# Two products of constants behind each step of the first eight heads, and late lower parts on VectorE

## The chip, the core and the metric

The kernel runs on one core of a Trainium2 chip. The metric is the device time of one execution in microseconds (us). TensorE (PE) runs the matrix products, with its weight loads shown apart (PEld), ScalarE (ACT) the activations and casts, VectorE (DVE) and GpSimd (POOL) the elementwise work, and SyncE (SP) issues every DMA. Each engine works through its own queue in order.

## What is computed

Attention with a memory term for 8 batches and 8 heads (576 tokens, 64 dimensions a head), and on its result a feed-forward layer with SiLU over 4608 tokens (512 to 2048 to 512).

```python
scores = scale * np.matmul(q, k.transpose(0, 1, 3, 2))          # causal mask, row maximum taken off
a = np.exp(scores); a /= a.sum(-1, keepdims=True) + 1e-09
local = np.matmul(a, v)
mem_out = (phi(q) @ M_prev) / (phi(q) @ z_prev + 1e-06)
x = g * mem_out + (1 - g) * local                                # g = sigmoid(beta), one a head
h = x @ w_in                                                     # [4608, 512] x [512, 2048]
out = (h * sigmoid(h)) @ w_out                                   # [4608, 2048] x [2048, 512]
```

## The kernel before

`attention()` is a generator that walks over the 64 heads. For head n it advances `scores` of head n and `values` of head n-1 by one step each per call; ten such steps make a head. `scores` transposes keys and queries on DVE (tile `tt`), lets PE make the scores of four query blocks (L250) and of the last one in two halves (L271), lets DVE mask them and take the row minimum of the negated scores (L252, L284), and ACT take the exponentials (L254, L294). POOL scales the rows (L304). `values` turns these blocks round on PE (L376, L393, L384), ACT copies them out (L401), and PE multiplies them with the memory and the values (L414, L422) into the bank `x`.

The first ten heads (`N_WHOLE`) are made in plain float32: every product of theirs appears as two records of PE. The later heads and the feed-forward layer work in split float32r parts.

Beside the heads, `preparation()` splits the weights, 32 pieces in all, three for every nine steps: for each piece three instructions of DVE on 128x512 (L152, L154, L159), two of POOL (L156, L162) and three of ACT. `ffn()` starts to be written out once the first eight heads are done (`done[0] >= H`), and then takes its share of steps beside the remaining heads. It works in 18 units of 256 tokens. In each unit the hidden activations of 256 columns (bank `h`, L552) pass ACT (tanh, L563), DVE (L564), ACT (upper part `hi`, L567) and POOL (lower part `lo` = th - hi, L568), and then enter the second product (bank `acc`, L532).

The final order of each engine's instructions is made by the framework's scheduler, which starts from the written order and uses a timeline of its own; `tc.issue_after(x)` keeps an instruction behind `x`. So any added instruction moves others as well. The pool `ps_a` holds two banks for `acc`.

Of the kernel before, what the change touches and what calls it, by code (L numbers as in the profile page):

```python
# [33 lines left out]
FFN_RATE = 0.22  # L34
FIRST_RATE = 0.2
FIRST_UNITS = 2
W_EARLY = 2


@with_exitstack  # L40
def memory_attention_then_silu_ffn(ctx, tc, q, k, v, M_prev, z_prev, beta, w_in, w_out, out):
# [173 lines left out]
    def scores(b, h, raw, rest, made, whole):  # L215
# [29 lines left out]
        for i in range(NQ - 1):  # L245
            w = P * i + P
            pt = pool.tile([P, w], F32, tag=f"p{i}", name=f"p{i}", bufs=P_BUFS)
            s = ps_s.tile([P, 512], F32, tag="s", name="s")[:, 0:w]
            for j, (ta, tb) in enumerate(terms):
                nc.tensor.matmul(  # L250
                    s, ta[:, P * i:P * i + P], tb[:, 0:w], start=j == 0, stop=j == len(terms) - 1)
            anchor["dve"] = nc.vector.tensor_tensor_reduce(  # L252
                s, s, mask[:, 3 * P - P * i:], QS, 3.0e38, ALU.add, ALU.min, st[:, i:i + 1]).ins
            nc.scalar.activation(  # L254
                pt, s, AF.Exp, bias=st[:, i:i + 1], scale=-1.0, accum_out=st[:, 10 + i:11 + i])
            pb.append(pt)
            yield
# [82 lines left out]
    def values(b, h, made, xs, whole):  # L340
# [24 lines left out]
        for lo, n, groups in ((0, SPLIT, ((0, 1),)), (SPLIT, HI, ((0, 3), (1, 4), (2,)))):  # L365
            x = ps_x.tile([P, 512], F32, tag="x", name="x")
            started = False
            for group in groups:

                t = ps_t.tile([P, 512], F32, tag="t", name="tp")  # L370
                o, spans = 0, []
                for j in group:
                    q0 = max(P * j, lo)
                    spans.append((j, o, q0 - lo))
                    for i in range(q0 // P, min((lo + n) // P, NQ - 1)):
                        nc.tensor.transpose(t[:, o:o + P], pb[i][:, P * j:P * j + P], ident)  # L376
                        o += P
                    if lo:
                        o += LAST
                if lo:  # L380

                    last, w = pb[-1], o // 2
                    if len(group) == 1:
                        nc.tensor.matmul(  # L384
                            t[:, o - LAST:o + LAST], last[:, 0:P], swapped,
                            start=True, stop=True, is_transpose=True)
                    else:
                        dst = t[:, o - 2 * LAST:o].rearrange("p (a b) -> p a b", b=LAST)
                        if group[1] == NQ - 2:
                            w = HI - P  # L390
                            dst = t[:, o - 2 * w:o].rearrange("p (a b) -> p a b", b=w)[:, :, w - LAST:]
                        c = P * group[0] + P
                        nc.tensor.matmul(  # L393
                            dst, last[:, c:c + P], ident.rearrange("p (a b) -> p a b", b=LAST),
                            start=True, stop=True, is_transpose=True)

                cut = o if group[-1] < NQ - 1 else o - LAST
                ph = pool.tile([P, 512], kind, tag="ph", name="ph", bufs=NB["ph"])
                pp = [ph]
                if whole:  # L400
                    nc.scalar.copy(ph[:, 0:cut], t[:, 0:cut])  # L401
                    if cut < o:
                        nc.scalar.copy(ph[0:LAST, cut:o], t[0:LAST, cut:o])
                else:
                    pl = pool.tile([P, 512], F32R, tag="pl", name="pl", bufs=NB["pl"])
                    nc.scalar.copy(ph[:, 0:o], t[:, 0:o])  # L406
                    nc.vector.tensor_tensor(out=pl[:, 0:cut], in0=t[:, 0:cut], in1=f(ph[:, 0:cut]), op=ALU.subtract)  # L407
                    if cut < o:
                        low = ph[LAST:P, cut:o]
                        nc.vector.tensor_tensor(out=low, in0=t[LAST:P, cut:o], in1=f(low), op=ALU.subtract)  # L410
                    pp.append(pl)
                yield
                if not started:
                    nc.tensor.matmul(x[0:rows, 0:n], ms, qp[:, lo:lo + n], start=True, stop=False)  # L414
                    started = True
                for part in pp:
                    for j, o, q0 in spans:
                        if part is not ph and j == NQ - 1:
                            continue
                        last = part is pp[-1] and group is groups[-1] and j == group[-1]  # L420
                        n_k = LAST if whole and j == NQ - 1 else P
                        nc.tensor.matmul(  # L422
                            x[0:rows, q0:n], vs[0:n_k, j], part[0:n_k, o:o + n - q0], start=False, stop=last)
            if whole:
                nc.scalar.copy(xs[own, lo:lo + n], x[0:64, 0:n])
                yield
                continue
            xb = pool.tile([P, HI], F32, tag="xb", name="xb", bufs=NB["xb"])
            nc.scalar.copy(xb[own, 0:n], x[oth, 0:n])
            nc.vector.tensor_tensor(out=xs[own, lo:lo + n], in0=x[own, 0:n], in1=xb[own, 0:n], op=ALU.add)  # L430
            yield

    xt = {}
    done = [0]

    def attention():
        todo = [(b, h) for b in range(B) for h in range(H)]
# [11 lines left out]
        for n in range(len(todo) + 1):  # L449

            first, made = iter(()), {}
            if n < len(todo):
                first = scores(*todo[n], raws.pop(0), rests.pop(0), made, n < N_WHOLE)
            one = two = True
            m = 0
            while one or two:
                for _ in range(FIRST_STEPS):
                    one = one and next(first, "end") != "end"
                if two and next(second, "end") == "end":
                    two = False  # L460
                    done[0] = n
                if m == 2 and n + 2 < len(todo):
                    raws.append(load_raw(*todo[n + 2]))
                m += 1
                yield
            if n < len(todo):
                b, h = todo[n]
                if n + 2 < len(todo):
                    rests.append(load_rest(*todo[n + 2]))
                if h % 2 == 0:  # L470
                    xt[b, h // 2] = pool.tile([P, S], F32, tag=f"xt{h // 2}", name="xt", bufs=2)
                second = values(b, h, made, xt[b, h // 2], n < N_WHOLE)
# [40 lines left out]
    def ffn():  # L513
# [3 lines left out]
        for u in range(NU):  # L517
# [21 lines left out]
            for p in range(NP):  # L539
# [25 lines left out]
                g = pool.tile([P, 2, 2, T], F32R, tag="g", name="g", bufs=G_BUFS)  # L565
                hi, lo = (g[:, j].rearrange("p c t -> p (c t)") for j in range(2))
                nc.scalar.copy(hi, th)  # L567
                nc.gpsimd.tensor_tensor(out=lo, in0=th, in1=f(hi), op=ALU.subtract)  # L568
                while not {("o", 2 * p), ("o", 2 * p + 1)} <= ready:
                    yield "prepare"  # L570
                before = p, g
# [63 lines left out]
```

## Time and profile before

| | |
|---|---|
| median of 3 runs | 1319.43 us (1318.79 to 1319.77) |
| profiled execution | 1320.44 us device time, span 1318.7 us |
| mean granted clock of PE | 0.971 |
| busy of the span | PE 1272.7 us, DVE 873.2 us, ACT 883.9 us, POOL 868.5 us |

The span runs from the first to the last instruction; 1.7 us lie outside it. A granted clock of 1.00 stands for 2.4 GHz, 0.50 for 1.2 GHz; a value between is a mean over a stretch with both. A busy PE is not PE at its peak: a product that runs at the lower clock is busy for longer. Where the records hold no change of the clock yet, the view shows 1.00; the length of the products themselves then tells the clock.

### The profile page before, as it was taken

The numbers are of one execution on the slowest core, as the hardware profiler recorded it, in microseconds if no ns is written. First come the engines' busy times: TensorE is split into PE (matmuls) and PEld (weight loads), VectorE is DVE, ScalarE is ACT, GpSimd is POOL, SyncE is SP. The second block draws the span as 40 slices with busy tenths as digits, with TensorE's granted clock in tenths as the row PEclk, the third lists the DMA queues.
The fourth block names the chain that finished last, engine by engine and source line by source line (L and its number), as shares of the span: only waits on it lengthen the run. The fifth ranks groups of instructions, "written<-read, shape, count | busy, mean of one in ns | idle before, by whom it ended". The sixth has DMA issues, their size and how long they took to land.

```text
span 1318.7 us, 24662 instructions
## 1 busy us (share of the span) xinstructions
PE 1272.7 (97%) x7858; PEld 1085.1 (82%) x7858; DVE 873.2 (66%) x2436; ACT 883.9 (67%) x2143; POOL 868.5 (66%) x1169
## 2 busy tenths in 40 slices
PE   6989899999999999999999999999999999999998
PEld 2334358888999989998988989899898998998887
DVE  7988874778777778787877777777767674111111
ACT  6777776777787777777777777777777774232222
POOL 6888895777777777777777777777767763221221
PEclk9976679999999999999999999999999999999999
DMA  6766555555455555555455555554545432444444
GB/s 165 190 181 169 158 133 163 141 134 144 127 147 144 138 153 138 153 137 143 133 147 141 136 141 148 137 153 135 156 126 150 121 116 86 154 160 131 144 157 144
DMA packets 302994, 190.39 MB, mean 144 GB/s; under 512 B 258832, under 2 KB 267024, under 8 KB 302864
## 3 DMA queue, kind: packets, MB, share of 16 engines
q1 hardware_dynamic: 302864, 188.82, 51.5%
q8 instruction: 62, 1.02, 0.3%
q14 instruction: 68, 0.56, 0.1%
HBM read 173.02 MB, written 15.73 MB: 143 GB/s over the span
## 4 chain that ended last, share of the span: by engine, by line
PE 73%; DVE 10%; ACT 6%; DMA 3%; issue 3%; POOL 2%; SPq 1%; POOLq 0%; DVEq 0%; ACTq 0%
PE h L552 27%; PE acc L532 24%; PE x L422 7%; PE s L250 5%; PE tp L376 4%; PE x L414 2%; PE tq L351 1%; DVE pl L407 1%; DVE s L252 1%; DVE th L564 1%; ACT p L254 1%; ACT th L563 1%; PE s L274 1%; DVE st L290 1%; DVE tt L221 1%
## 5 line engine op out<-in xcount | busy, mean ns | idle before, releaser
L552 PE MATMUL h<-xu,wi 128*128 128x256 f32 x2592 | 377.7, 287 | 9.3 <-DVE th L564 7.2
L552 PEld LDWEIGHTS h<-xu,wi 128*128 128x128 f32 x2592 | 342.9, 191 | 25.1 <-DVE th L564 9.4
L568 POOL TENSOR_TENSOR g<-th,g 128x512 fp32r<-128x512 f32 x144 | 186.6, 1297 | 203.5 <-ACT g L567 200.2
L532 PE MATMUL acc<-wo,g 128*128 128x512 f32 x864 | 244.7, 398 | 0.2 <-POOL g L568 0.2
L304 POOL TENSOR_SCALAR p<-p,st 128x384 f32<-128x384 f32 (+3 forms) x320 | 182.5, 590 | 76.7 <-DVE st L302 73.7
L532 PE MATMUL acc<-flow,g 128*128 128x512 f32 x864 | 231.2, 394 | 1.3 <-DMA flow<-wo_s 1.3
L564 DVE SCALAR_TENSOR_TENSOR th<-th,h 128x512 f32<-128x512 f32 x144 | 98.4, 684 | 180.3 <-ACT th L563 178.4
L532 PEld LDWEIGHTS acc<-flow,g 128*128 128x128 f32 x864 | 158.8, 188 | 34.4 <-DMA flow<-wo_s 1.8
L254 ACT ACTIVATE p<-s,st 128x128 f32<-128x128 f32 (+3 forms) x256 | 134.9, 528 | 70.7 <-DVE st L252 53.5
L532 PEld LDWEIGHTS acc<-wo,g 128*128 128x128 f32 x864 | 148.7, 189 | 19.7 <-POOL g L568 0.6
L563 ACT ACTIVATE th<-h 128x512 f32<-128x512 f32 x144 | 85.9, 597 | 99.2 <-PE h L552 98.7
L407 DVE TENSOR_TENSOR pl<-tp,ph 128x384 fp32r<-128x384 f32 x216 | 118.6, 551 | 36.0 <-ACT ph L406 32.7
L252 DVE CUSTOM_DVE_ANT_0 s<-s,mask 128x128 f32<-128x128 f32 (+3 forms) x256 | 125.2, 492 | 23.5 <-PE s L250 20.0
L376 PE MATMUL tp<-ident,p 128*128 128x128 f32 x640 | 121.0, 290 | 3.2 <-POOL p L304 2.6
L552 PE MATMUL h<-xu,flow 128*128 128x256 f32 x864 | 122.4, 283 | 0.0
L406 ACT CAST ph<-tp 128x384 fp32r<-128x384 f32 x216 | 104.7, 490 | 26.1 <-PE x L422 21.2
L567 ACT CAST g<-th 128x512 fp32r<-128x512 f32 x144 | 89.2, 620 | 49.1 <-DVE th L564 48.3
L552 PEld LDWEIGHTS h<-xu,flow 128*128 128x128 f32 x864 | 113.1, 191 | 2.3 <-issue 0.3
L376 PEld LDWEIGHTS tp<-ident,p 128*128 128x128 f32 x640 | 81.5, 146 | 27.5 <-POOL p L304 7.2
L422 PE MATMUL x<-pl,vs 128*128 128x256 f32 x324 | 82.1, 308 | 1.0 <-DVE pl L407 0.9
L232 POOL TENSOR_TENSOR kk<-tt,kk 64x576 fp32r<-64x576 f32 x54 | 77.3, 1431 | 5.0 <-ACT kk L230 1.2
L235 POOL TENSOR_TENSOR ql<-tt,qq 64x512 fp32r<-64x512 f32 x54 | 69.8, 1293 | 15.1 <-ACT qq L231 6.7
(103 smaller groups left out, 2399.6 us busy)
## 6 DMA issues: line engine op xcount, KB each, us to landing
flow<-wo_s SPq DMA_DIRECT2D x144, 512.0 KB, 3.6
flow<-wi_s SPq DMA_DIRECT2D x72, 512.0 KB, 3.8
raw<-in_k SPq DMA_DIRECT2D x128, 72.0 KB, 2.5
raw<-in_q SPq DMA_DIRECT2D x128, 72.0 KB, 2.8
out<-o SPq DMA_DIRECT2D x36, 256.0 KB, 4.2
wraw<-in_moe_w_in SPq DMA_DIRECT2D x16, 512.0 KB, 4.4
qn<-in_q SPq DMA_DIRECT2D x64, 128.0 KB, 2.8
vr<-in_v SPq DMA_DIRECT2D x64, 128.0 KB, 2.5
```

The source lines that it names most:

```text
L252: anchor["dve"] = nc.vector.tensor_tensor_reduce(s, s, mask[:, 3 * P - P * i:], QS, 3.0e38, ALU.add, ALU.min, st[:, i:i + 1]).ins
L254: nc.scalar.activation(pt, s, AF.Exp, bias=st[:, i:i + 1], scale=-1.0, accum_out=st[:, 10 + i:11 + i])
L304: nc.gpsimd.tensor_scalar(pb[x], pb[x], st[:, 15 + x:16 + x], 1.0, op0=ALU.mult, op1=ALU.mult)
L376: nc.tensor.transpose(t[:, o:o + P], pb[i][:, P * j:P * j + P], ident)
L406: nc.scalar.copy(ph[:, 0:o], t[:, 0:o])
L407: nc.vector.tensor_tensor(out=pl[:, 0:cut], in0=t[:, 0:cut], in1=f(ph[:, 0:cut]), op=ALU.subtract)
L422: nc.tensor.matmul(x[0:rows, q0:n], vs[0:n_k, j], part[0:n_k, o:o + n - q0], start=False, stop=last)
L532: nc.tensor.matmul(acc[t], ta, tb, start=p == 0 and c == 0 and n == 0, stop=p == NP - 1 and c == 1 and n == len(terms) - 1)
L552: nc.tensor.matmul(h[:, c], ta, tb, start=kk == 0 and n == 0, stop=kk == KD - 1 and n == len(terms) - 1)
L563: nc.scalar.activation(th, h, AF.Tanh, scale=0.5)
L564: nc.vector.scalar_tensor_tensor(out=th, in0=th, scalar=1.0, in1=h, op0=ALU.add, op1=ALU.mult)
L568: nc.gpsimd.tensor_tensor(out=lo, in0=th, in1=f(hi), op=ALU.subtract)
```

## The change

1. `keep_busy` puts two products of 128 x 128 x 128 (float32, the stationary operand is the identity `ident`, the moving one the first 128 columns of `mask`, which are zeros) behind each step of `attention()` while n < 8. They write a bank `idle`, taken from `ps_a` ahead of everything else, which nobody reads. Each pair is kept behind the product that `anchor["pe"]` named before the step. The first two steps of head 0 have no such anchor, so there are 78 pairs, 156 products.
2. Where all heads are written out (`done[0] == B * H`), the lower part of the activated sum is made on DVE and not on POOL: 36 of the 144.

```diff
+WARM = 2
@@ scores: the four query blocks
-                nc.tensor.matmul(
-                    s, ta[:, P * i:P * i + P], tb[:, 0:w], start=j == 0, stop=j == len(terms) - 1)
+                anchor["pe"] = nc.tensor.matmul(
+                    s, ta[:, P * i:P * i + P], tb[:, 0:w], start=j == 0, stop=j == len(terms) - 1).ins
@@ values: the product with the values
-                        nc.tensor.matmul(
-                            x[0:rows, q0:n], vs[0:n_k, j], part[0:n_k, o:o + n - q0], start=False, stop=last)
+                        anchor["pe"] = nc.tensor.matmul(
+                            x[0:rows, q0:n], vs[0:n_k, j], part[0:n_k, o:o + n - q0], start=False, stop=last).ins
+    def keep_busy(behind):
+
+        for _ in range(WARM):
+            with tc.issue_after(behind):
+                nc.tensor.matmul(idle[:, 0:P], ident, mask[:, 0:P], start=True, stop=True)
+
+    idle = ps_a.tile([P, DM], F32, tag="a", name="idle")
@@ attention: each step
+                behind = anchor.get("pe")
                 for _ in range(FIRST_STEPS):
                     one = one and next(first, "end") != "end"
...
+                if behind and n < H:
+                    keep_busy(behind)
@@ ffn
-                nc.gpsimd.tensor_tensor(out=lo, in0=th, in1=f(hi), op=ALU.subtract)
+                late = nc.vector if done[0] == B * H else nc.gpsimd
+                late.tensor_tensor(out=lo, in0=th, in1=f(hi), op=ALU.subtract)
```

What the scheduler makes of it on PE at the very start, the scores of head 0 (`s`, with `tt` and `qf` the keys and queries) and the turning of its feature map (`tq`). Before:

```order
L250 MATMUL s<-tt,qf 128x256
L250 MATMUL s<-tt,qf 128x384
L250 MATMUL s<-tt,qf 128x512
L271 MATMUL s<-tt,qf 64x256
L351 MATMUL tq<-ident,e 128x128 x2
L351 MATMUL tq<-ident,e 64x128
L271 MATMUL s<-tt,qf 64x320
```

And now, where L251 is the old L250, L272 the old L271, L352 the old L351 and L438 an added product:

```order
L251 MATMUL s<-tt,qf 128x256
L438 MATMUL idle<-mask,ident 128x128 x4
L251 MATMUL s<-tt,qf 128x384
L438 MATMUL idle<-mask,ident 128x128 x2
L251 MATMUL s<-tt,qf 128x512
L438 MATMUL idle<-mask,ident 128x128 x10
L272 MATMUL s<-tt,qf 64x256
L438 MATMUL idle<-mask,ident 128x128 x2
L352 MATMUL tq<-ident,e 128x128 x2
L352 MATMUL tq<-ident,e 64x128
L438 MATMUL idle<-mask,ident 128x128 x2
L272 MATMUL s<-tt,qf 64x320
```

Sixteen added products stand ahead of the first half of head 0's last block, four more ahead of the second half.

The same engine where the fourth head begins its turning (`tp` turns blocks `p`, `x` takes products with the values `vr`). Before:

```order
L422 MATMUL x<-ph,vr 64x64
L351 MATMUL tq<-ident,e 128x128 x2
L351 MATMUL tq<-ident,e 64x128
L271 MATMUL s<-tt,qf 64x256
L271 MATMUL s<-tt,qf 64x320
L250 MATMUL s<-tt,qf 128x128
L422 MATMUL x<-ph,vr 64x320
L250 MATMUL s<-tt,qf 128x256
L376 MATMUL tp<-ident,p_654 128x128
```

And now (L423 is the old L422, L377 the old L376):

```order
L423 MATMUL x<-ph,vr 64x64
L438 MATMUL idle<-mask,ident 128x128 x2
L352 MATMUL tq<-ident,e 128x128 x2
L352 MATMUL tq<-ident,e 64x128
L272 MATMUL s<-tt,qf 64x256
L423 MATMUL x<-ph,vr 64x320
L438 MATMUL idle<-mask,ident 128x128 x12
L272 MATMUL s<-tt,qf 64x320
L251 MATMUL s<-tt,qf 128x128
L377 MATMUL tp<-ident,p_713 128x128
```

Twelve of a head's twenty added products stand behind the last product with the values, ahead of the second half of the next scores; the other eight stand in pairs among the turned blocks. The last product with the values has moved ahead of that second half.

The end of PE's queue, the last unit of the feed-forward layer. Before:

```order
L532 MATMUL acc<-wo_142,g 128x512 x6
L552 MATMUL h<-xu,flow 128x256 x12
L532 MATMUL acc<-flow,g 128x512 x6
L532 MATMUL acc<-wo_144,g 128x512 x6
L532 MATMUL acc<-flow,g 128x512 x6
```

And now (L564 is the old L552, L544 the old L532):

```order
L564 MATMUL h<-xu,flow 128x256 x12
L544 MATMUL acc<-wo_142,g 128x512 x6
L544 MATMUL acc<-flow,g 128x512 x6
L544 MATMUL acc<-wo_144,g 128x512 x6
L544 MATMUL acc<-flow,g 128x512 x6
```

Twelve products of the sum before now lie between the last hidden activations and the products that use them, where there were six.

## Rows read from the trace of the kernel before

**Rows 1.** The page: busy tenths and granted clock in 40 slices of 33 us.
```profile
PE   6989899999999999999999999999999999999998
DVE  7988874778777778787877777777767674111111
PEclk9976679999999999999999999999999999999999
```
**Rows 2.** Windows: length, busy of PE, PEld, DVE, ACT, POOL, then clock, DMA share, GB/s.
```profile
16.30:66.10 49.80, 46.19 (x101) 18.42 (x101) 44.31 (x107) 36.97 (x89) 40.18 (x36) 1.00 0.71 190
66.10:176.10 110.00, 98.30 (x286) 44.85 (x285) 95.84 (x213) 83.05 (x201) 93.99 (x86) 0.68 0.58 160
198.00:1318.70 1120.70, 1100.20 (x7354) 1004.06 (x7352) 709.31 (x2049) 740.52 (x1801) 700.91 (x994) 1.00 0.50 141
```
**Rows 3.** Timeline of PE: start, length, what, and the idle time before it with its releaser.
```profile
66.08 0.55 PE L351 MATMUL tq<-ident,e 128*128 128x128 f32 x3
...
76.29 1.87 PE L422 MATMUL x<-ph,vr 128*64 128x320 f32 x8
78.09 0.55 PE L351 MATMUL tq<-ident,e 128*128 128x128 f32 x3
79.65 0.64 PE L271 MATMUL s<-tt,qf 64*64 64x256 f32 x2 [1.01 <-ACT p L254]
80.67 0.75 PE L271 MATMUL s<-tt,qf 64*64 64x320 f32 x2 [0.38 <-ACT p L254]
85.20 0.79 PE L250 MATMUL s<-tt,qf 64*128 64x128 f32 x2 [3.77 <-DVE st L284]
...
98.53 3.44 PE L422 MATMUL x<-ph,vr 128*64 128x320 f32 x8
101.90 0.90 PE L351 MATMUL tq<-ident,e 128*128 128x128 f32 x3
...
116.96 3.37 PE L422 MATMUL x<-ph,vr 128*64 128x320 f32 x8
120.26 0.55 PE L351 MATMUL tq<-ident,e 128*128 128x128 f32 x3
```
**Rows 4.** Windows between changes of the clock, columns as in rows 2.
```profile
82.60:103.00 20.40, 17.80 (x44) 8.60 (x45) 19.96 (x43) 15.45 (x35) 18.02 (x18) 0.50 0.74 208
106.60:120.00 13.40, 13.40 (x35) 6.52 (x35) 11.74 (x24) 9.15 (x24) 10.88 (x9) 0.50 0.50 126
```
**Rows 5.** Timeline of PE, later.
```profile
172.76 3.44 PE L422 MATMUL x<-ph,vr 128*64 128x320 f32 x8
176.12 0.90 PE L351 MATMUL tq<-ident,e 128*128 128x128 f32 x3
...
178.00 3.57 PE L552 MATMUL h<-xu,wi 128*128 128x256 f32 x15
```
**Rows 6.** Waits of DVE, 16.3 to 176.1: us in total, times, longest.
```profile
DVE pair L284 <- PE s L271: 10.3, 10, 1.8
DVE s L252 <- PE s L250: 3.1, 4, 1.6
```
**Rows 7.** Timeline of PE at the start.
```profile
10.30 3.35 PE L250 MATMUL s<-tt,qf 64*128 64x384 f32 x4 [1.67 <-ACT p L254]
13.89 1.11 PE L271 MATMUL s<-tt,qf 64*64 64x256 f32 x2 [0.25 <-ACT p L254]
16.32 0.90 PE L351 MATMUL tq<-ident,e 128*128 128x128 f32 x3 [1.31 <-POOL e L334]
```
**Rows 8.** Groups by shape: busy, mean ns, idle before. POOL from 1090, DVE 198 to 1090.
```profile
L568 POOL TENSOR_TENSOR g<-th,g 128x512 fp32r<-128x512 f32 x37 | 47.8, 1295 | 154.9 <-ACT g L567 154.8
L407 DVE TENSOR_TENSOR pl<-tp,ph 128x512 fp32r<-128x512 f32 x52 | 35.4, 681 | 2.7 <-ACT ph L406 2.2
```
**Rows 9.** Timeline of the end, all engines.
```profile
1311.54 1.29 POOL L568 TENSOR_TENSOR g<-th,g 128x512 fp32r<-128x512 f32 x1 [5.62 <-ACT g L567]
...
1312.89 0.74 PE L532 MATMUL acc<-wo,g 128*128 128x512 f32 x2 [0.17 <-POOL g L568]
```

## The prediction

> **What bounds the kernel now.** I read the slices of the page first: PE is busy nine tenths or more of nearly every slice, but its granted clock is below full in slices 3 to 6, and PE and DVE both have gaps in the first six [rows 1]. So the span falls into two parts. From 198 us to the end PE is busy 1100.2 of 1120.7 us at a clock of 1.00 [rows 2]: this part is bound by PE, both edits leave its useful products alone, and it is shorter only if it starts sooner. The first part, 16.3 to 176.1 us, makes the first eight heads in 159.8 us. There PE is busy 46.2 + 98.3 = 144.5 us, DVE 44.3 + 95.8 = 140.2 us and POOL 40.2 + 94.0 = 134.2 us [rows 2], so three engines lie within 8% of each other and none is the clear bound.
>
> But PE's 144.5 us are swollen. The eight products with the values take 3.37 us from start to start (98.53 to 101.90) in one head and 1.80 us (76.29 to 78.09) in another [rows 3]: the factor 1.87 is the clock. In 82.6 to 103.0 and 106.6 to 120.0 the granted clock is 0.50, that is 1.2 GHz [rows 4]. From one turning of the feature map to the next (the L351 rows) the fast head takes 78.09 - 66.08 = 12.0 us, the next one 101.90 - 78.09 = 23.8 us, of which 5.2 us are waits [rows 3].
>
> What PE did before the clock moved: it rose at 103 and at 120 us, each time behind the run of eight products with the values (98.53, 116.96), which load all 128 rows of the array, and it fell after the waits of 1.01, 0.38 and 3.77 us that lie between 78.6 and 85.2 us [rows 3, 4]. Such a run does not always do it: the one at 172.76 is followed by another slow turning, 0.90 us as at 101.90, not 0.55 [rows 3, 5]. Being busy alone did not raise the clock either: from 106.6 to 120.0 PE was busy 13.40 of 13.40 us at 0.50 [rows 4]. The Trainium skill (TensorE: Matmul & The Clock Gate, Part 1) says that the array is throttled by default and that sustained activity releases it. Read as busy time, the trace differs: that stretch was all busy and stayed at 0.50. By the page alone, filler would have nothing to lift there and would only cost, which is the third rival's sum.
>
> **The change, part by part.**
>
> *The price of one added product.* No product of this shape stands in the trace. The nearest rows are the runs of eight, seven times 128 columns in two passes each (320, 192, 320 and 64 columns): 1.80 / 7 = 0.26 us at full clock, 3.37 / 7 = 0.48 us at half [rows 3]. So 156 products cost 41 us of PE at full clock and 75 us at half. Both ends are kept; I take 0.26, except at the start. Unlike the products with 64 rows (the `64*64` and `64*128` rows), the added ones load 128 x 128, as the turned blocks do. That the moving operand is all zeros has no row; the turned blocks move the identity, which is nearly all zeros, and are not set apart by any row.
>
> *The clock, 16.3 to 176.1 us.* I take it that the added products, which close the gaps and load all rows, hold the clock high for most of this part. Then the eight heads are 8 x 12.0 = 96 us of PE, and the 138 added products that are left for this part (18 of the 156 stand ahead of the first turning) 138 x 0.26 = 36 us: 132 us, against 144.5 before. DVE with 140.2 us is then the most loaded engine, and what the change is worth is what DVE stops waiting for. DVE idles 159.8 - 140.2 = 19.6 us in this part, and PE ends 10.3 + 3.1 = 13.4 us of it [rows 6]. This is the upper bound of the gain. The lower bound is below nothing (second rival). Since PE turns from the most loaded engine into one with 28 us of room, I take two thirds of 13.4: **-9 us**. The rest I leave, because twelve of a head's twenty products stand straight ahead of the second L271 half, for whose result DVE's L284 waits.
>
> *The start.* At the start the clock is low: at 10.30 two blocks of 384 and 512 columns take 3.35 us [rows 7], and 896 columns in two passes take 3.37 us in the slow run above. Four added products, 4 x 0.48 = 1.9 us, fall into the wait of 1.67 us ahead of 10.30. Two and ten more, 12 x 0.48 = 5.8 us, stand ahead of the first L271, which began at 13.89 [rows 7]. Behind it the wait of 1.31 us (L351) gives some of it back, and if the clock rises inside the run of ten, the rest is shorter. Bounds 0 and 5.8; I take half: **+3 us**.
>
> *The lower part on DVE.* On POOL one takes 1295 ns; DVE's nearest subtraction of the same size, with one operand in PSUM, takes 681 ns [rows 8]. The 0.6 us of each count only where PE waits: at the end that is 0.17 us, at 1312.89 [rows 9]. Everywhere else the next block's products cover the chain. Bounds 0 and -0.6; I take **-0.2 us**. DVE has the room: its slices at the end are 1 tenth busy [rows 1]. Twelve products instead of six now lie between the last hidden activations and their use, which covers that chain as well, so nothing new is late there.
>
> *The bank and the order.* `idle` holds one of two `acc` banks, but its last product stands in PE's own queue ahead of head 8, before any sum is begun: 0. Each anchor also moves other instructions. For the order after 198 us the bound is PE's idle time there, 1120.7 - 1100.2 = 20.5 us; I put a few us either way into the range and none into the sum. No DMA is added; loads come a little earlier with the heads.
>
> *The sum:* -9 + 3 - 0.2 = -6.2 us on the profiled execution's 1320.4 (span 1318.7 and 1.7 around it) is 1314.2. That execution stands 1.0 above the median of the runs, 1319.4, so the forecast is **1313 us**.
>
> **The rivals.**
>
> *1. What the clock gives, the filler takes: about 1319.* DVE is busy 19.96 of 20.40 us in the slow stretch from 82.6 [rows 4], so there a faster PE gives almost nothing. If this is the rule, the -9 shrinks to -3 and the start takes it back. Against it: in 106.6 to 120.0 DVE has 1.7 of 13.4 us idle.
>
> *2. Slower, because a run of twelve stands ahead of what DVE needs: 1332.* PE now idles 159.8 - 144.5 = 15.3 us in this part, 1.9 us a head; the twelve are 3.1 us at full clock and 5.8 at half. What exceeds the wait that stood there delays L271, then L284 and, DVE being in order, the weight pieces and row minima queued behind it. At 3.1 - 1.9 = 1.2 us for each of eight heads that is 10 us, with 3 at the start 13 us. It decides as soon as the twelve cost more than about 2 us a head net. For it: the wait of 3.77 us in front of L250 is ended by L284, so delay on PE and delay on DVE feed each other. Against it: that same wait is the place that the run fills.
>
> *3. The products do not lift the clock: 1365.* Then they cost 75 us, less the 15.3 us of waits and some 12 us at the start that can hold them: +45 us or more. For it: the zeros, and 13.4 us of full busyness at 0.50.
>
> *4. The whole of DVE's waits goes and the start is free: 1306.* -13.4 and 0.
>
> **How the numbers follow.** Forecast (1307 to 1316) 0.42, rival 4 0.10, rival 1 0.20, rival 2 0.20, rival 3 0.08. A measurement of this kernel tells 0.2%, 2.6 us, from no change. Faster by more than that: 0.42 + 0.10 = 0.52; same: 0.20; slower: 0.20 + 0.08 = 0.28. The range 1303 to 1335 leaves out about 0.04 below and 0.15 above (rival 3 and the upper third of rival 2).
>
> **What the profile after would show.** Right: L438 in runs of eight to twelve at 0.26 us each; a granted clock of 0.9 or more in slices 3 and 4; the runs of eight at 1.8 us; DVE's waits for L271 and L250 at a third of 13.4 us; the first big block of L552 products, now at 178.0 us [rows 5], some 6 us earlier and everything behind it shifted alike. Wrong: added products of 0.48 us with the clock at 0.50 (rival 3); L284's wait for L271 longer than 10.3 us (rival 2); DVE's idle time unchanged with PE at full clock (rival 1); the stretch from the first big L552 block to the end longer or shorter than before by more than 3 us, in which case the order, which I put at nothing, had a price.

## The result and the profile after

The changed kernel took 1328.28 us (median of 4 runs, 1325.14 to 1329.22) against 1319.11 us for the kernel before on the same chip (4 runs, 1318.03 to 1319.77). The ratio is 1.0057, 95% interval 1.0037 to 1.0077: slower, where I forecast 1313 us and faster. Of every kernel's executions, one more than 1.5% above its fastest is left out; that is one of the six of e8 below. The profiled execution took 1327.76 us, with a span of 1325.7 us and a mean granted clock of 0.983 (before: 0.971).

The page of the kernel after, in 40 slices of 33 us, to hold against [rows 1]:

```profile
PE   7999979999999999999999999999999999999998
DVE  6999984778687768777776767767867775322222
PEclk9799989999999999999999999999999999999999
```

The clock did what I had forecast: slices 3 to 6 were 7, 6, 6 and 7 tenths, and are now 9, 9, 9 and 8. Windows of the kernel after, between turnings of the feature map (columns as in [rows 2]):

```profile
20.96:65.69 44.73, 41.59 (x166) 24.10 (x165) 40.54 (x90) 32.87 (x78) 35.10 (x31) 0.77 0.72 189
65.69:171.72 106.03, 99.42 (x499) 59.11 (x497) 99.33 (x210) 81.50 (x194) 95.84 (x84) 0.97 0.62 177
171.72:198.33 26.61, 19.74 (x92) 13.89 (x90) 20.51 (x50) 17.10 (x42) 23.76 (x28) 0.81 0.39 96
198.33:1325.70 1127.37, 1105.91 (x7376) 1009.76 (x7374) 732.88 (x2089) 743.62 (x1806) 654.88 (x959) 1.00 0.50 140
```

From the turning of head 2 to that of head 8 the clock is 0.97 (before 0.68 [rows 2]). The eight heads take 44.73 + 106.03 = 150.76 us from the first turning to the ninth, against 159.8: 9.0 us less. But the next step, from the turning of head 8 to that of head 9, takes 26.61 us, of which PE is busy 19.74 us. The same step of the kernel before, in one window:

```profile
176.12:193.36 17.24, 17.24 (x89) 11.89 (x88) 12.29 (x32) 11.77 (x31) 16.91 (x19) 0.84 0.62 165
```

There PE was never idle. So of the 9.4 us that this step grows by, 6.9 us are PE's idle time and 2.5 us longer busy time. I cut the two spans at five marks: the turnings of heads 0, 8 and 9, the thirteenth output copied out of `acc` by ACT (at 662.36 us before and 672.49 us after), and the end. The loss is then 4.6 us ahead of the first turning, -9.0 in the eight heads, +9.4 from turning 8 to turning 9, +5.2 from there to the thirteenth output (474.2 us, not 469.0, of which PE is idle 9.7 and not 7.0) and -3.1 from there to the end (653.2 us, not 656.3): +7.0 us, as the spans have it.

Timeline of PE of the kernel after at that step, where the feed-forward layer comes in (L564 is the old L552):

```profile
169.92 1.87 PE L423 MATMUL x<-ph,vr 128*64 128x320 f32 x8
171.72 0.55 PE L352 MATMUL tq<-ident,e 128*128 128x128 f32 x3
174.00 0.39 PE L564 MATMUL h<-xu,wi 128*128 128x256 f32 x1 [1.73 <-ACT xu L516]
176.68 3.20 PE L564 MATMUL h<-xu,wi 128*128 128x256 f32 x14 [2.28 <-DVE xu L517]
179.81 0.97 PE L272 MATMUL s<-tt,qf 64*64 64x256 f32 x4
...
185.68 1.73 PE L564 MATMUL h<-xu,wi 128*128 128x256 f32 x12 [2.86 <-DVE th L576]
...
198.33 0.55 PE L352 MATMUL tq<-ident,e 128*128 128x128 f32 x3
```

And of the kernel before, at the same place:

```profile
176.95 1.11 PE L271 MATMUL s<-tt,qf 64*64 64x256 f32 x2
...
181.49 0.77 PE L271 MATMUL s<-tt,qf 64*64 64x320 f32 x2
...
185.90 1.68 PE L552 MATMUL h<-xu,wi 128*128 128x256 f32 x12
...
193.36 0.55 PE L351 MATMUL tq<-ident,e 128*128 128x128 f32 x3
```

After the change both halves of the scores of head 8 (L272) stand behind the fifteen L564 products, and these wait for `xu`: 1.73 + 2.28 us. Before, the first half stood ahead of them (176.95). Twelve more L564 products wait 2.86 us for `th`. These three waits are the 6.9 us that PE is idle. What DVE does meanwhile, in its timeline:

```profile
168.47 1.75 DVE L155 SCALAR_TENSOR_TENSOR wy<-wraw,wy 128x512 uint32<-128x512 uint32 x1
...
170.54 1.78 DVE L155 SCALAR_TENSOR_TENSOR wy<-wraw,wy 128x512 uint32<-128x512 uint32 x1
...
172.31 0.68 DVE L160 SCALAR_TENSOR_TENSOR wy<-wraw,wy 128x512 f32<-128x512 f32 x1
...
176.14 1.46 DVE L517 TENSOR_TENSOR xu<-xt,xu 128x256 fp32r<-128x256 f32 x3
...
180.71 0.42 DVE L285 CUSTOM_DVE_ANT_0 pair<-s,mask 64x256 f32<-64x256 f32 x1 [1.49 <-PE s L272]
...
194.67 0.57 DVE L253 CUSTOM_DVE_ANT_0 s<-s,mask 128x384 f32<-128x384 f32 x1 [3.94 <-PE s L251]
```

And `xu` on DVE in the kernel before (L517 is the old L505):

```profile
175.15 0.56 DVE L505 TENSOR_TENSOR xu<-xt,xu 128x256 fp32r<-128x256 f32 x1
...
176.24 2.13 DVE L505 TENSOR_TENSOR xu<-xt,xu 128x256 fp32r<-128x256 f32 x2
```

Here PE has come early and DVE has not. Turning 8 comes 4.4 us sooner than before, but pieces of the weights, row minima and row sums stand ahead of `xu` in DVE's queue. DVE begins `xu` at 176.14 us, where it began at 175.15 before, and is done with it at 177.6 us (176.14 + 1.46), where it was done at 178.4. So PE's lead of 4.4 us ends in 4.0 us of waiting for `xu`, and the half of the scores that filled the time before stands behind it now. Then DVE waits 1.49 and 3.94 us for scores that stand behind the L564 products on PE.

DVE's waits for PE in the eight heads, to hold against [rows 6] (13.4 us in all):

```profile
DVE pair L285 <- PE s L272: 5.2, 5, 1.7
DVE s L253 <- PE s L251: 1.1, 2, 0.8
```

They are 6.3 us, 7.1 us less. DVE's idle time in the eight heads fell from 19.6 to 10.9 us (150.76 - 40.54 - 99.33), and its busy time stayed (139.9 and 140.2 us). The start, against [rows 7], and the added products of the whole kernel as one group (two records each, so 156 products in 52.7 us):

```profile
8.54 2.07 PE L438 MATMUL idle<-mask,ident 128*128 128x128 f32 x8
...
15.28 4.63 PE L438 MATMUL idle<-mask,ident 128*128 128x128 f32 x20
19.84 0.64 PE L272 MATMUL s<-tt,qf 64*64 64x256 f32 x2
...
20.96 0.49 PE L352 MATMUL tq<-ident,e 128*128 128x128 f32 x3
```

```profile
L438 PE MATMUL idle<-mask,ident 128*128 128x128 f32 x312 | 52.7, 316 | 0.0
```

Of these, the ones in the eight heads (busy of PE and PEld, clock, DMA share, GB/s):

```profile
20.96:171.72 150.76, 44.24 (x278) 36.98 (x276) 0.91 0.65 181
```

And the late lower part on DVE, against [rows 8, 9]: its group, and the last of them with the products that use it.

```profile
L581 DVE TENSOR_TENSOR g<-th,g 128x512 fp32r<-128x512 f32 x36 | 24.9, 695 | 22.4 <-ACT g L579 22.3
```

```profile
1317.92 0.69 DVE L581 TENSOR_TENSOR g<-th,g 128x512 fp32r<-128x512 f32 x1 [0.69 <-ACT g L579]
...
1319.08 1.54 PE L544 MATMUL acc<-wo,g 128*128 128x512 f32 x6
```

### The profile page after: what moved, and what is told of

Its sections match the earlier page's. It is cut to its first block, busy times and chain, and to the rows that moved or that the text cites. A ratio compares the mean times of both kernels' runs of the same rounds, so it can differ in the third digit from the quotient of the medians.

```text
span 1325.7 us, 25266 instructions
## 1 busy us (share of the span) xinstructions
PE 1280.6 (97%) x8170; PEld 1116.6 (84%) x8170; DVE 904.1 (68%) x2472; ACT 885.6 (67%) x2143; POOL 824.9 (62%) x1133
## 4 chain that ended last, share of the span: by engine, by line
PE 72%; DVE 12%; ACT 5%; POOL 4%; DMA 3%; issue 3%; SPq 0%; POOLq 0%; DVEq 0%; ACTq 0%
PE h L564 28%; PE acc L544 24%; PE x L423 6%; PE s L251 5%; PE tp L377 4%; PE idle L438 1%; DVE st L291 1%; DVE wy L155 1%; PE x L415 1%; PE tq L352 1%; DMA flow<-wo_s 1%; DVE s L253 1%; DVE wy L160 1%; DVE wy L153 1%; POOL p L305 1%
## 5 line engine op out<-in xcount | busy, mean ns | idle before, releaser
L564 PE MATMUL h<-xu,wi 128*128 128x256 f32 x2592 | 377.7, 288 | 12.8 <-DVE th L576 8.1
L564 PEld LDWEIGHTS h<-xu,wi 128*128 128x128 f32 x2592 | 343.2, 191 | 28.0 <-DVE th L576 7.9
L544 PE MATMUL acc<-wo,g 128*128 128x512 f32 x864 | 242.4, 397 | 0.0
L544 PE MATMUL acc<-flow,g 128*128 128x512 f32 x864 | 231.8, 395 | 1.1 <-DMA flow<-wo_s 1.1
L544 PEld LDWEIGHTS acc<-flow,g 128*128 128x128 f32 x864 | 158.3, 188 | 34.0 <-DMA flow<-wo_s 2.4
L581 POOL TENSOR_TENSOR g<-th,g 128x512 fp32r<-128x512 f32 x108 | 140.3, 1299 | 49.8 <-ACT g L579 48.4
L544 PEld LDWEIGHTS acc<-wo,g 128*128 128x128 f32 x864 | 149.2, 188 | 19.4 <-POOL p L308 0.5
L564 PE MATMUL h<-xu,flow 128*128 128x256 f32 x864 | 126.2, 287 | 0.0
L377 PE MATMUL tp<-ident,p 128*128 128x128 f32 x640 | 117.2, 280 | 1.8 <-ACT ph L402 0.8
L564 PEld LDWEIGHTS h<-xu,flow 128*128 128x128 f32 x864 | 115.9, 195 | 2.3 <-issue 0.8
L377 PEld LDWEIGHTS tp<-ident,p 128*128 128x128 f32 x640 | 80.2, 143 | 17.6 <-POOL p L305 2.1
L423 PE MATMUL x<-pl,vs 128*128 128x256 f32 x324 | 82.1, 308 | 2.5 <-DVE pl L408 2.4
```

Of the source, the lines that this page charges most:

```text
L423: anchor["pe"] = nc.tensor.matmul(x[0:rows, q0:n], vs[0:n_k, j], part[0:n_k, o:o + n - q0], start=False, stop=last).ins
L544: nc.tensor.matmul(acc[t], ta, tb, start=p == 0 and c == 0 and n == 0, stop=p == NP - 1 and c == 1 and n == len(terms) - 1)
L564: nc.tensor.matmul(h[:, c], ta, tb, start=kk == 0 and n == 0, stop=kk == KD - 1 and n == len(terms) - 1)
L581: late.tensor_tensor(out=lo, in0=th, in1=f(hi), op=ALU.subtract)
```

## The experiments

Twelve kernels ran, four to a batch, each with five rounds against the kernel before (medians 1319.4, 1319.3 and 1319.5 us in the three batches). Behind the scheduler an instruction that nobody counts on can be taken out or put in while every other one keeps its place; so products and order can be told apart.

**e1: the late edit alone.**

```diff
-                nc.gpsimd.tensor_tensor(out=lo, in0=th, in1=f(hi), op=ALU.subtract)
+                late = nc.vector if done[0] == B * H else nc.gpsimd
+                late.tensor_tensor(out=lo, in0=th, in1=f(hi), op=ALU.subtract)
```

> Only the second edit: no products, no idle bank; the lower part on VectorE once all heads are written out. In the changed kernel the outputs of the units lag those of before by 10.7 us at 1134 us and by 7.0 us at the end, so 3.7 us were won behind 1134 us. Theory A (the late edit and the order of the tail that comes with it win by themselves): 1316 us, 1315 to 1317. Theory B (the lag shrank because the late start had left slack that the tail took back): 1319, no difference to before.

Measured: 1317.64 us, ratio 0.9979 (0.9967 to 0.9992). By the ratio that is -2.8 us, not -0.2 (between the medians 1.8). The order is that of before up to 1106 us; from there on the edit and the new order of the tail come together, so this is the price of both. In its profiled execution the stretch from the thirteenth output to the end is 652.6 us, against 656.3.

**e2: the products alone**, with the lower part left on POOL (the reverse of the diff of e1, in the changed kernel).

> Only the first edit: the 156 products and their bank; the lower part stays on GpSimd. Theory A (the two edits are independent): the changed kernel's time plus the 3 us that the late edit wins, 1330 us, 1328 to 1332. Theory B (no gain from the late edit): 1327.

Measured: 1328.71 us, ratio 1.0075 (1.0059 to 1.0090). The products and what they bring carry the whole loss.

**e3: the order of the changed kernel without its products.** Taken out behind the scheduler: 137 of the 156, all on which no other instruction counts.

```diff
+    mine = [n for n, i in enumerate(rows) if i.opcode == "Matmult" and "idle" in i.outs[0].memref]
+    free = [n for n in mine if rows[n].sync_info is None]
+    for n in reversed(free):
+        del rows[n]
```

> The changed kernel with 137 of its 156 products taken out behind the scheduler, so that every engine keeps the order of the changed kernel; the 19 left are those whose count other engines wait for. Theory O (the new order of the useful work is what costs, above all where the feed-forward layer begins): as slow as the changed kernel or slower, 1325 to 1333, with the granted clock at 0.50 again in the heads and the waits for xu and th at 172 to 186 us still there. Theory P (the products' own time on TensorE costs): back at 1314 to 1319.

Measured: 1327.63 us, ratio 1.0059 (1.0037 to 1.0081). The loss is all there without the products. In its trace (1331.14 us, the longest of its six) the clock over the eight heads is 0.70, and they take 164.6 us; with the products (after) it was 0.91 and 150.8 us. Against e1 the spans differ by 12.1 us (1329.4 and 1317.3), of which 8.8 us lie in the step from turning 8 to 9 (24.0 and 15.1 us) and 2.8 us between there and the thirteenth output. In that step PE, never idle in e1, is idle 4.5 us, for `xu` and `th`, and busy 4.3 us longer, at a clock of 0.79 in place of 0.99. So in this order the held clock does shorten the heads, by 14 us in these two executions. But with the products the first turning is 4.6 us later, the step from turning 8 to 9 takes 26.6 and not 24.0 us, and the stretch behind it is 2.3 us longer; 3.7 us are left between the two spans (1329.4 and 1325.7), and nothing between the medians. The bank `idle` is taken here too, so this run does not tell it from the order; but e6 and e9 below take it as well and are faster than before.

**e4: the products in the order of the kernel before**, 136 of them put in behind their anchors once it had been scheduled, from the first turning on, into a bank that is free then.

```diff
...
+    for name in sorted(new, key=place.get, reverse=True):
+        for i in new[name]:
+            rows.insert(place[name] + 1, i)
```

> The kernel before in its own order on every engine, with 136 of the products put in behind the scheduler, each directly behind the product that the changed kernel ties it to, from the first turning of head 0 on (the pairs ahead of it are left out). They write the bank of the first sum, free then. Theory O (the order costs, the clock gains): 1313 to 1318, clock near 1.00 in the heads and the feed-forward layer beginning a few us before 178. Theory P (the products' time costs): 1322 to 1330. Theory F (VectorE and GpSimd set the pace of the first heads, so that a faster TensorE gives nothing): 1318 to 1321 with the clock near 1.00 and VectorE's waits for TensorE gone but its instructions longer.

Measured: 1328.11 us, ratio 1.0065 (1.0049 to 1.0080). Here the products themselves are at fault: 8.7 us in the order of before. Waits of DVE in the eight heads, which take 170.5 us (L286, L273, L254 and L252 are the old L284, L271, L252 and L250):

```profile
DVE pair L286 <- PE s L273: 17.4, 9, 6.0
DVE s L254 <- PE s L252: 9.3, 6, 3.0
```

That is 26.7 us, twice the 13.4 of [rows 6]: my second rival, in an order that the scheduler had not made for the products.

**e5: 84 products only where PE waited**, in the order of e1.

```diff
+                if i == 0 and j == 0 and 2 <= H * b + h <= H:
+                    AHEAD[made_now.name] = 8
...
+                if x0 == 0 and 1 <= H * b + h < H:
+                    AHEAD[made_now.name] = 4
...
+            rows.insert(place[name], i)
```

> The order of the kernel before (with the late edit), 84 products put in behind the scheduler only where PE waited in its trace: four ahead of the first L271 half of heads 1 to 7 and eight ahead of the first L250 block of heads 2 to 8, 84 x 0.26 = 22 us of PE. Left out against the whole change: the products among the turned blocks and the scheduler's new order. Step 1's theory (the clock held high shortens PE, DVE stops waiting, and the end follows): the late edit's 1317.6 less 5 to 9, 1308 to 1313, clock 0.98 or more. Theory D (DVE and POOL set the pace of the early heads, so a faster PE gives the end nothing): 1316 to 1319, the clock risen all the same. Theory P (products in the old order delay what DVE waits for): 1321 to 1328, DVE's waits for L250 and L271 longer than 13.4 us.

Measured: 1316.70 us, ratio 0.9977 (0.9968 to 0.9987), within the interval of e1. The products cost nothing there, and give nothing: no part of the 5 to 9 us that my theory asked for. Theory D is the one that has this time, with the clock risen: of the nine turnings of heads 0 to 8 seven run at the full clock (0.49 or 0.55 us for the three products, 0.85 or 0.90 at half), three in e1. In the profiled executions the eight heads take 160.9 us against 164.0, a difference that two executions of one order can have (see below the table).

**e6: one product a step** (78), scheduled anew; **e7: products through ten heads** (196); **e8: products of 64 columns.**

```diff
-WARM = 2
+WARM = 1
```

> The change with one product a step and not two (78 in all), scheduled anew. Theory per product (each product costs): half of the loss, 1322 to 1324. Theory O (the loss is the price of the order that the scheduler made, and any other order has a price of its own, not in proportion to the products): not bound to half; 1314 to 1332, and if it falls outside 1321 to 1325 it speaks for O. In its trace the turning of head 8 and of head 9 tell where: O expects the difference in single turnings, not evenly over the eight heads.

```diff
-                if behind and n < H:
+                if behind and n < N_WHOLE:
```

> The change with products behind the steps of the first ten heads and not eight (196 in all). Theory E (the 9.3 us lost between the turnings of heads 8 and 9 come from the lower clock and the waits of PE there, which more products would close): the step from turning 8 to turning 9 falls from 26.6 to about 18 to 20 us, the clock there 0.95 or more, and the time is 1319 to 1323. Theory O (the order at the entry to the feed-forward layer is what costs, products or not): 1326 to 1333, with the clock risen and the step still 24 us or more.

```diff
-                nc.tensor.matmul(idle[:, 0:P], ident, mask[:, 0:P], start=True, stop=True)
+                nc.tensor.matmul(idle[:, 0:P // 2], ident, mask[:, 0:P // 2], start=True, stop=True)
```

> The change with products of 64 columns and not 128, scheduled anew: as many products in about the same places, but some 20 us of PE less in all. Theory per column (PE's time in the products is the price): 1319.4 + 4 to 5, about 1324. Theory O (the order is the price): the time is that of its own order, which differs from the change's in a third of PE's rows: 1316 to 1332, not bound to 1324. Theory D (DVE and POOL set the pace): the eight heads from turning 0 to turning 8 take 148 to 154 us as in the change, though PE has 20 us less to do.

Measured: e6 1312.96 us, ratio 0.9950 (0.9936 to 0.9964); e7 1334.42, ratio 1.0115 (1.0098 to 1.0132); e8 1332.09 (five executions, 1329.53 to 1343.01), ratio 1.0125 (1.0088 to 1.0162). Half the products do not cost half the loss: the kernel is 6 us faster than before, 4.7 us faster than e1, which no price per product can do. Theory E fails too: in e7 the step from turning 8 to 9 is still 24.9 us, and PE is idle in it 1.9 us and no longer 6.9. The clock there is 0.86, not the 0.95 of the theory.

e8 is not the test that I had meant, since a product of 64 columns is not cheaper than one of 128. In e8, eight products (two records each) at the full clock, and twelve at half:

```profile
85.57 2.00 PE L438 MATMUL idle<-mask,ident 128*128 128x64 f32 x16
...
164.86 5.38 PE L438 MATMUL idle<-mask,ident 128*128 128x64 f32 x24
```

That is 0.25 and 0.45 us a product; twelve of 128 columns in the changed kernel take 0.25 each:

```profile
86.54 2.94 PE L438 MATMUL idle<-mask,ident 128*128 128x128 f32 x24
```

And they held the clock less well: the turnings of heads 0, 1 and 6 run at half, and the eight heads take 180.8 us in the profiled execution, one of its two long ones (1343.0 us). So e8 has an order of its own and part of its filler at the lower clock, a piece of my third rival, and tells nothing of either alone.

What e6 does at the entry, on PE and then on DVE:

```profile
169.47 0.90 PE L352 MATMUL tq<-ident,e 128*128 128x128 f32 x3
170.02 2.48 PE L564 MATMUL h<-xu,wi 128*128 128x256 f32 x15
172.43 0.76 PE L272 MATMUL s<-tt,qf 64*64 64x256 f32 x4
...
185.07 0.55 PE L352 MATMUL tq<-ident,e 128*128 128x128 f32 x3
```

```profile
168.77 1.25 DVE L517 TENSOR_TENSOR xu<-xt,xu 128x256 fp32r<-128x256 f32 x3
```

The same fifteen L564 products stand ahead of the same L272, but `xu` is written by 170.0 us, 7.6 us sooner than in the changed kernel (2.3 us of that are the earlier turning), and PE does not wait for it. The step takes 15.6 us, and the eight heads 151.2, as in the change.

**e9: the order of e6 with 62 of its 78 products taken out**, as in e3.

> The kernel with one product a step (1313.0 us), its order kept on every engine, with 62 of its 78 products taken out behind the scheduler (16 stay, on which others count). Theory O (that order is what is better): with the products gone the time stays near 1313, 1310 to 1316. Theory C (it is the clock, held high by few products in the gaps): the clock falls back in slices 3 to 6 and the time goes to 1316 to 1322, that of before or of the late edit alone.

Measured: 1312.72 us, ratio 0.9961 (0.9946 to 0.9975). The clock did fall back, as theory C asks (the middle of its executions has a mean granted clock of 0.973, of e6 0.979, of the kernel before 0.975), and the time did not: the order alone is what is better in e6. Against e1 this is 4.9 us between the medians, but the intervals of the two ratios overlap (0.9946 to 0.9975, 0.9967 to 0.9992). Its profiled execution was the longest of its 12, 1321.3 us, so its row in the table below says little of the others.

**e10 to e12: products for head 0 alone (16), for head 7 alone (20), for heads 4 to 7 (80).** The diff of e10; the others have `n == 7` and `4 <= n < H`.

```diff
-                if behind and n < H:
+                if behind and n == 0:
```

> The change with products behind the steps of head 0 alone: 16 products, 4 to 8 us of PE, most of them in the wait at the start; but the scheduler's order differs from that of the late edit alone in some 2960 rows of PE. Theory per product: the late edit's 1317.6 plus 1 to 3, 1318 to 1321, with a first turning later by 1 to 4 us and nothing else. Theory O: a time of its own, anywhere from 1308 to 1336; outside 1314 to 1324 it can be no price of 16 products.

> The change with products behind the steps of head 7 alone: 20 products, 5 us at the full clock, and the order of before up to turning 7 (it differs from the late edit's in some 800 rows of PE from there on). Theory per product: 1317.6 plus 0 to 5. Theory O: turnings 0 to 7 as in the kernel before within 4 us, and what differs comes at the entry to the feed-forward layer or behind it; the time 1310 to 1332.

> The change with products behind the steps of heads 4 to 7: 80 products, the order of before up to turning 4, and only some 290 rows of PE differ from the late edit's in all. Theory C (the clock is worth something where the order stays): heads 4 to 7 take 4 to 8 us less than the 74 to 76 us of before and the time is 1310 to 1315. Theory D (VectorE and GpSimd set the pace of these heads): 1316 to 1320. Theory P (the products delay VectorE): 1321 to 1326.

Measured: e10 1338.34 us, ratio 1.0145 (1.0131 to 1.0160); e11 1319.90, ratio 1.0010 (0.9997 to 1.0022), which decides nothing; e12 1327.74, ratio 1.0064 (1.0046 to 1.0081). A kernel with sixteen more products, all over by 20 us, is 19 us slower: no price of theirs can do that. That it is their order is so concluded and not shown, since no run has this order without them. The clock of e10 is as low as before (0.66 over the eight heads; before 0.68 from the turning of head 2 on), and PE waits for `xu` at the entry as in the change:

```profile
PEclk8675679999999999999999999999999999999999
```

```profile
174.35 0.38 PE L564 MATMUL h<-xu,wi 128*128 128x256 f32 x1
178.01 3.36 PE L564 MATMUL h<-xu,wi 128*128 128x256 f32 x14 [3.27 <-DVE xu L517]
...
200.13 0.55 PE L352 MATMUL tq<-ident,e 128*128 128x128 f32 x3
```

e12 lies in none of the ranges of its three theories. It has the order of before up to turning 4 and from there on another, on DVE above all, so its heads 4 to 7 hold the clock, the 80 products and a new order together. Window of e12 from turning 4 to turning 8, and below it that of the kernel before:

```profile
103.73:177.66 73.93, 68.49 (x324) 39.76 (x322) 56.92 (x127) 52.22 (x127) 55.59 (x52) 0.91 0.54 153
```

```profile
101.90:176.12 74.22, 67.86 (x191) 30.84 (x190) 63.95 (x143) 55.47 (x135) 64.42 (x59) 0.66 0.54 150
```

A clock of 0.91 in place of 0.66, and the same 74 us: PE is busy 68 us either way, in e12 20.6 us of it with the added products. What the clock gave, the filler took, as my first rival said, here with room left on DVE. But the changed kernel has the same 80 products there and takes 67.4 us (104.28 to 171.72), so in another order it is not so. What e12 loses against e1 lies in the step from turning 8 to 9 (24.0 and 15.1 us). Among its twelve executions the shortest (1320.8 us) has the highest mean clock (0.992) and the longest (1333.8 us) the lowest (0.983); which of the two is the cause, no run tells.

**All kernels at the same marks** (us of the profiled executions; `late` says whether the late edit is in, "full clock" how many of the turnings 0 to 8 run at the full clock):

| kernel | late | full clock | first turning | heads 0 to 7 | turning 8 to 9 | to the 13th output | to the end |
|---|---|---|---|---|---|---|---|
| before | no | 4 | 16.3 | 159.8 | 17.2 | 469.0 | 656.3 |
| after | yes | 9 | 21.0 | 150.8 | 26.6 | 474.2 | 653.2 |
| e1 | yes | 3 | 16.4 | 164.0 | 15.1 | 469.1 | 652.6 |
| e2 | no | 9 | 21.0 | 150.7 | 26.5 | 471.8 | 655.1 |
| e3 | yes | 5 | 16.4 | 164.6 | 24.0 | 471.9 | 652.6 |
| e4 | no | 6 | 16.6 | 170.5 | 15.1 | 469.3 | 654.9 |
| e5 | yes | 7 | 16.4 | 160.9 | 16.5 | 468.7 | 652.5 |
| e6 | yes | 7 | 18.3 | 151.2 | 15.6 | 472.9 | 653.3 |
| e7 | yes | 8 | 21.2 | 156.3 | 24.9 | 478.4 | 652.4 |
| e8 | yes | 6 | 20.8 | 180.8 | 17.1 | 469.8 | 652.5 |
| e9 | yes | 5 | 16.6 | 159.5 | 17.1 | 473.4 | 652.8 |
| e10 | yes | 5 | 20.2 | 152.6 | 27.3 | 478.0 | 659.4 |
| e11 | yes | 4 | 16.3 | 161.9 | 19.4 | 472.4 | 652.5 |
| e12 | yes | 6 | 16.3 | 161.3 | 24.0 | 468.8 | 653.4 |

e1 has the order of before in its first three columns and differs by 4 us in the second, so a difference of that size there is that of two executions. The column "turning 8 to 9" falls into two groups, 15 to 17 us and 24 to 27 us, with e11, which is neither faster nor slower, between them. All of the second (after, e2, e3, e7, e10, e12) are slower than before; of the first, only e4 and e8 are, and they lose it in the eight heads. In every kernel of the second group PE waits for DVE's `xu` at the first large block of L564, 1.7 to 3.5 us; in none of the first group, nor in e11, does it wait there. The number of turnings at the full clock goes with neither group.

## Why the prediction was wrong, step by step

- **The step that failed: "The bank and the order", which I put at nothing.** With the late edit and with 19 of the 156 products left, the new order takes 1327.63 us (e3); the late edit alone 1317.64 (e1). So the order costs 10.0 us, more than the whole change does. The 19 are not it: they all lie ahead of turning 8, where e3 is as fast as e1 (first turning 16.4 us in both, then 164.6 and 164.0 us). I had bounded "the order after 198 us" by PE's idle time there, and had looked for runs of products ahead of L271 up to 176 us; the place that costs most is the one between, 176 to 198 us, which stands in none of my terms. My list of signs did name it: the stretch from the first big L552 block to the end, longer by more than 3 us, is 8.3 us longer (from 178.00 us before, from 176.68 us after).
- **The clock, -9 us.** The mechanism is as I said: the clock rose to 0.97, DVE's waits for PE fell by 7.1 us of 13.4 (to 6.3 us, not to my third, 4.5), and the eight heads took 9.0 us less. But none of it is found at the end. In three pairs of runs with the same order, the products leave the time where it was: 1327.63 without and 1328.28 with them (e3, after), 1312.72 and 1312.96 (e9, e6), 1317.64 and 1316.70 (e1, e5); of the turnings at full clock there are 5 and 9 in the first pair, 3 and 7 in the last. In the fourth (before, e4) they cost 8.7 us, with 4 and 6 such turnings. In the first pair the heads won 14 us in the profiled executions, and the start (4.6 us), the step at the entry (2.6 us) and the stretch behind it (2.3 us) took most of it back; at the entry PE is earlier than the engine that feeds it. One reading was off and enters no term: the clock fell at 82.6 us, inside the wait of 3.77 us (81.4 to 85.2) and not behind it. That the -9.0 matches the forecast to the decimal says little: the same stretch is 152.6 us in e10, at a clock of 0.66.
- **The price of a product, 0.26 us.** 0.25 us at the full clock, as I took it, but 52.7 / 156 = 0.34 us on the mean: in the eight heads 44.2 us where I had put 36, since some ran at the lower clock.
- **The start, +3 us:** +4.6 us, within its bounds of 0 and 5.8.
- **The late edit, -0.2 us, was mis-sized:** -2.8 us (-1.1 to -4.4 by the interval of e1), with the order of the tail that comes with it. The lower part went from 1295 to 695 ns as forecast. I counted one wait at the very end; the stretch from the thirteenth output to the end is 1.5 to 4 us shorter in every kernel with the edit but e10 than in those without it. In which of its blocks those microseconds lie, and whether the edit or the order of the tail wins them, is open.
- **The rivals.** The first (the filler takes what the clock gives) is what heads 4 to 7 of e12 look like, in an order of their own, and not those of the change. The second (runs of twelve delay DVE) is true of the old order (e4) and not of the scheduler's own, where DVE's waits fell; that its 1332 us lies nearest to the measured time is chance. The third (the clock is not lifted) is out by the page of the profile after. A rival that was missing: the scheduler's answer to more products anywhere is a new order for all that follows, and the kernels made so lie between -5 us (e6, e9) and +21 us (e10) of e1.
- **What stays open:** why the scheduler puts the pieces of the weights ahead of `xu` in one order and behind it in another, and how much of the 10 us that one place is. The step from turning 8 to 9 has 9.4 of the 19.2 us (4.6 + 9.4 + 5.2) that the profiled execution lost, and 8.8 of the 12.1 us between those of e1 and e3; what stretches the part behind it (5.2 us in the change, 2.8 in e3) was not followed. Moving `xu` alone was not tried, since other engines count on each instruction around it.

The best kernel of the study is e6, or e9 with the same order: 0.995 and 0.996 of the time before, from an order found by chance and the late edit.

## What to carry to other kernels

Where a scheduler writes the order, an edit has two prices, that of the added work and that of the new order, and the second can be the larger by far: sixteen products came with 19 us here, and another order was 5 us faster than e1. Hold the order and change the work, then hold the work and change the order, before believing either; and put the spread of a few harmless variants into the range of the forecast. Here an engine that was made faster ahead of a hand-over waited there for what the other side did not have ready: look at the first wait behind the stretch, not only at the stretch.

## What the runs showed of the hardware

That products whose moving operand is all zeros and whose results nobody reads raise the granted clock was open ahead of the run; it rose from 0.68 to 0.97 over six heads, and with the order held (e3, after) from 0.70 to 0.91 over eight (in e3 the first 20 us of these lie ahead of the first record of the clock and count as 1.00).

The same instruction of DVE takes from 0.67 to 1.70 us. In the kernel before, one line of the weight pieces from 16.3 to 176.1 us (shortest, middle and longest in ns):

```profile
L154 DVE SCALAR_TENSOR_TENSOR wy<-wraw,wy x29: 674/741/1699, 24.2 to 170.3; 128x512 uint32<-128x512 uint32 x29
```

In the rows of the changed kernel above, where it is L155, it starts at 168.47 and at 170.54 and takes 1.75 and 1.78 us; POOL's rows at these times are

```profile
168.32 1.35 POOL L236 TENSOR_TENSOR ql<-tt,qq 64x512 fp32r<-64x512 f32 x1
...
170.48 1.29 POOL L157 TENSOR_TENSOR wy<-wy,wraw 128x512 uint32<-128x512 uint32 x1
```

Both times POOL starts up to 0.15 us ahead of it and ends (169.67, 171.77) some 0.55 us before DVE does, as if DVE's own 0.6 us began only then; L160 of the same size takes 0.68 us from 172.31, just ahead of POOL's next instruction, and then it is this one that takes 1.75 and not 1.29 us:

```profile
172.40 1.75 POOL L157 TENSOR_TENSOR wy<-wy,wraw 128x512 uint32<-128x512 uint32 x1 [0.63 <-DVE nrm L332]
```

The Trainium skill (GPSIMD Engine Reference, Specifications) says that POOL shares its way to the state buffer with DVE and gets in the way of DVE instructions with two inputs from there; these rows agree. So DVE's 140 busy us in the first part, which I took for work, seem to hold waits for POOL that no view lists as waits: with every one of the 29 at the shortest 0.67 us, L154 alone would take 8.6 us less. By that, an order that sets the two side by side makes DVE slower without any added work; how much of the change's loss this is, no run tells, and DVE's busy time in the eight heads did not grow (139.9 and 140.2 us).
